# Batch 0's opening of an attention-and-MLP kernel, issued from a written list of pieces

## The chip, the cores and the metric

The kernel runs on one core of one Trainium2 chip. A core has a matrix engine (TensorE, PE in the profile, with weight loads shown as PEld), a vector engine (VectorE, DVE), an activation engine (ScalarE, ACT), a general engine (GpSimd, POOL), and a queue engine (SyncE, SP) that here only issues DMAs. Each engine runs its instructions in the order in which the program issued them and waits on semaphores for the others. PE writes to PSUM, which POOL can't read; DVE and ACT move results from there to SBUF.

The metric is the device time of one execution in microseconds (us). The kernel before took 324.24 us, the median of three runs (324.21 to 324.35).

## The reference

Sliding-window attention over 8 batches of 8 heads, 576 tokens and 64 channels, and then a two-layer perceptron with a leaky ReLU on the 4608 tokens.

```python
scores = (1.0 / np.sqrt(D)) * np.matmul(q, k.transpose(0, 1, 3, 2))     # [8, 8, 576, 576]
mask = np.abs(pos[:, None] - pos[None, :]) <= 32
scores = np.where(mask, scores, -1e9)
attn = exp(scores - max); attn = attn / (attn.sum(-1) + 1e-9)
x = np.matmul(attn, v).transpose(0, 2, 1, 3).reshape(4608, 512)
h = x @ w_in                       # [512, 2048]
out = np.maximum(0.01 * h, h) @ w_out   # [2048, 512]
```

Inputs are float32 and so is the output. The kernel computes in bf16.

## The kernel before

**Tiling.** Two heads make a pair, so each batch has four pairs `p`. A batch's 576 tokens are cut into two halves of 288 (`HALF`). An attention step `i` is one half of one pair: `i = 8*b + 4*half + p`. Steps 0 to 3 are batch 0's first half, steps 4 to 7 its second. The MLP goes by groups `g` of 288 tokens: group 0 needs steps 0 to 3, group 1 needs steps 4 to 7.

**Operands.** `qf`, `kf`, `vf` are float32 tiles as loaded; `qb` and `kb` their casts, 96 tokens on the partitions; `tp` a transposed pair in PSUM; `qT` the transposed queries. `kbd` and `vbd` hold keys and values block-diagonally, so that the two heads of a pair share one matmul; their off-diagonal blocks have to be cleared once. There are two copies of both, for even and odd batches. `win` and `mask` are the 0/1 window.

**One step** consists of: five score matmuls into the single PSUM tile `ps` (line 301); one exponential on ACT into `e` (306); a product with the mask on POOL into `prob` (308); two matmuls with a block of ones for the sums (333); a reciprocal on DVE (338); five matmuls of probabilities with values (352); and a scaling on DVE into `xT` (366). The functions are `score`, `sums`, `product` and `scaled`. There is one buffer for `ps`, one each for `s` and `x`, two for `e`, and four PSUM banks named `mm` that transposes, first-layer and second-layer results share; with `spare`, a step's sums or product take one of these instead.

**The MLP.** `h_tile(g, f)` makes 128 of the 2048 hidden columns: four matmuls over the four pairs of `xT` (line 380) and a Prelu on ACT into `gT` (387). `h_first` interleaves the first four tiles so that the matmuls of pair `c` can run as soon as that pair's `xT` is there. `o_tile` does the second layer (422), an eviction (427) and the store. `keep_busy` (434) issues matmuls whose results nobody reads.

**Order.** The program is in manual schedule: each engine's order is the order of the calls. From line 487 the opening of batch 0 is written out by hand: casts, transposes (`turn_over`, `transpose`, `straight`), masks, scores 0 to 3, then the products; first-layer tiles of group 0 are mixed with steps 4 to 7 in `second_half`. Then group 1's first layer runs while batch 1's queries and keys are cast and transposed (`second_pair`). From there a planner spreads the steps evenly between the MLP's matmuls, by `due` times in estimated microseconds.

**Queues.** SP issues the loads of queries, values and (after batch 0) keys, and the stores. POOL issues, between its computing instructions, DMAs that cast on the way: batch 0's four key loads (line 109), four slices of `w_in` (480) and four of `w_out` (484). `load_early` (101) issues query pair and key pair in turn. The value loads (93) wait on a one-element DVE memset (91), and batch 1's loads (79) on a POOL memset (75); everything behind such a wait on SP waits too.

The parts of the opening that the change touches most are the calls that begin with `cast_q(0, DVE)`:

```python
    cast_q(0, DVE)
    turn_over(0, 0, "q")
    tk0 = transpose(0, 0, "k")
    DVE.memset(kbd[0][:, 2:4], 0.0)
    cast_q(1, DVE)
    straight(0, tk0, ACT, DVE)
    turn_over(0, 1, "q")
    for p in range(NPAIR):
        load_v(0, p, DVE if p == 0 else None)
```

Of the kernel before, what the change touches and what calls it, by code (L numbers as in the profile page):

```python
# [12 lines left out]
ALU = mybir.AluOpType  # L13


@with_exitstack
def kernel(
# [85 lines left out]
    def load_early(p):  # L103

        t = fload.tile([96, 2, RUN * D], FP32, name=f"qf{p}")
        nc.sync.dma_start(out=t, in_=q[0, 2 * p:2 * p + 2].rearrange("a (p c) d -> p a (c d)", c=RUN))
        qf[0, p] = t
        t = kb[:, p].rearrange("p c a d -> p (c a d)").rearrange("p (a c d) -> p a c d", c=RUN, d=D)
        nc.gpsimd.dma_start(out=t, in_=k[0, 2 * p:2 * p + 2].rearrange("a (p c) d -> p a c d", c=RUN))
        early[p] = t  # L110
# [3 lines left out]
    for p in range(NPAIR):  # L114
        load_early(p)
# [13 lines left out]
    def clear(t, p):  # L129
        flat = t[:, p].rearrange("p n j -> p (n j)")  # L130
        nc.scalar.activation(
            out=flat, in_=zero.to_broadcast([128, NB * 128]), func=AF.Copy,
        )
# [14 lines left out]
    w = win[0:64]  # L148
    nc.gpsimd.affine_select(
        out=w, in_=w, compare_op=ALU.is_ge, fill=0.0,  # L150
        base=0, channel_multiplier=-1, pattern=[[1, 2], [0, 3], [2, 64]],
    )
    nc.gpsimd.affine_select(
        out=w, in_=w, compare_op=ALU.is_ge, fill=0.0,
        base=2 * W, channel_multiplier=1, pattern=[[-1, 2], [0, 3], [-2, 64]],
    )
    nc.gpsimd.memset(vbd[0][:, 2], 0.0)
    nc.gpsimd.memset(vbd[0][:, 3], 0.0)
    win_f = win.rearrange("p c m i -> p c (m i)")

    def make_mask(hf):
        lo = (16, 32)[hf]
        nc.vector.tensor_copy(out=mask[hf][:, 0], in_=win_f[:, :, lo:lo + EVEN])
        lo = (16, 0)[hf]
        nc.vector.tensor_copy(out=mask[hf][:, 1, :, lo:lo + 128], in_=win_f[:, :, 0:128])
# [10 lines left out]
    clear(vbd[0], 0)  # L176
    clear(vbd[0], 1)
# [43 lines left out]
    def transpose(b, p, which):  # L221
        tp = mmps.tile([128, RUN, 96], BF16, name="tp", tag="mm")
        for c in range(RUN):
            if b == 0 and which == "k":
# [13 lines left out]
    def straight(p, tp, *engs):  # L238

        for a, eng in enumerate(engs):  # L240
            r = slice(64 * a, 64 * a + 64)
            copy(eng, kbd[0][r, p, :, r], tp[r].rearrange("p c i -> p i c"))

    def cast_q(p, eng):
        copy(eng, qb[:, p], qf[0, p].rearrange("p a (c d) -> p c a d", d=D))

    def evict(b, p, which, tp):
        if which == "q":
            nc.scalar.activation(
                out=qT[b][:, p].rearrange("p (c i e) -> p c i e", c=2, e=RUN // 2),  # L250
                in_=tp.rearrange("p (e c) i -> p c i e", c=2), func=AF.Copy,
# [44 lines left out]
    def score(i):  # L296
        b, hf, p = where(i)
        by_c = qT[b][:, p].rearrange("p (c i) -> p c i", c=2)
        for n_, blocks in enumerate(WIN[hf]):
# [5 lines left out]
        e = attn.tile([128, 2 * HALF], BF16, name="e")  # L305
        nc.scalar.activation(out=e, in_=ps[:, P0:P0 + 2 * HALF], func=AF.Exp, scale=scale)  # L306
        pr = prob[:, i % NPROB]
        nc.gpsimd.tensor_mul(  # L308
            pr.rearrange("p n c i -> p (n c i)"), e, mask[hf].rearrange("p n c i -> p (n c i)"),
        )  # L310
        probs[i] = [pr, None, None]
# [9 lines left out]
    def sums(i, spare=False):  # L321

        b, hf, p = where(i)
        pr, both, _ = probs[i]
# [4 lines left out]
        if both is not None:  # L329
            nc.tensor.matmul(s, ones_bd, both, start=True, stop=True)  # L330
        else:
            for n in range(2):
                nc.tensor.matmul(  # L333
                    s, ones_bd, pr[:, n].rearrange("p c i -> p (c i)"),
                    start=(n == 0), stop=(n == 1),
                )
        r = recip.tile([128, HALF], FP32, name="r")
        nc.vector.reciprocal(r, s)  # L338
        probs[i][2] = r

    def product(i, spare=False):
# [3 lines left out]
        if spare:  # L345
            x = mmps.tile([128, 512], FP32, name="mm", tag="mm")[:, 0:HALF]
        else:
            x = xps.tile([128, HALF], FP32, name="x")
# [7 lines left out]
        probs[i][1] = x  # L356
# [7 lines left out]
    def scaled(i):  # L364
        _, x, r = probs.pop(i)
# [34 lines left out]

    def h_first(g):

        hs = [mmps.tile([128, 512], FP32, name="mm", tag="mm") for _ in range(4)]
        yield hs[0]
        for c in range(DMC):
            for f in range(4):
                h_mms(g, f, hs[f], (c,))
            if c == DMC - 1:
                for f in range(4):
                    h_out(g, f, hs[f])  # L410
            yield
# [75 lines left out]
    ACT, DVE, POOL = nc.scalar, nc.vector, nc.gpsimd  # L487
    cast_q(0, DVE)
    turn_over(0, 0, "q")
    tk0 = transpose(0, 0, "k")  # L490
    DVE.memset(kbd[0][:, 2:4], 0.0)
    cast_q(1, DVE)
    straight(0, tk0, ACT, DVE)
    turn_over(0, 1, "q")
    for p in range(NPAIR):
        load_v(0, p, DVE if p == 0 else None)
    cast_q(2, DVE)
    cast_q(3, POOL)
    DVE.tensor_copy(out=win[64:128], in_=win[0:64])
    make_mask(0)  # L500
    score(0)
    straight(1, transpose(0, 1, "k"), ACT, DVE)
    turn_over(0, 2, "q")
    make_mask(1)
    load_w_in(0, 512)
    score(1)
    sums(0)
    straight(2, transpose(0, 2, "k"), ACT, ACT)
    turn_over(0, 3, "q")
    tk3 = transpose(0, 3, "k")  # L510
# [171 lines left out]
```

## Time and profile before

| what | value |
|---|---|
| median of three runs | 324.24 us |
| the profiled execution | 323.54 us |
| its span, first to last instruction | 321.8 us |
| first transposes of queries on PE | 4.40 us |
| first scores, step 0 (line 301) | 9.27 us |
| first matmuls of line 380 | 25.42 us |
| memset that releases batch 1's loads (line 75) | 28.32 us |
| end of the last scaling of batch 0 (line 366) | 39.33 us |
| first matmuls of the second layer (line 422) | 48.25 us |
| PE busy in 12 to 16, 16 to 20, 20 to 24, 24 to 28 us | 3.94, 2.75, 2.38, 4.00 us |

The span counts from the first instruction to the last; the time of the run has 1.74 us more around it. A row of the instruction timeline gives start, length, engine, line, operation and tiles, and in brackets the idle time before it and what ended that. "PE busy" is modelled from pipelined matmuls, so a busy PE isn't PE at its best rate. The chain of waits follows the end of the span back, step by step, to what released each piece of work.

### The profile page before, as it was taken

What the parts mean: (1) busy time and instruction counts of PE and PEld (TensorE: products, weight loads), DVE (VectorE), ACT (ScalarE), POOL (GpSimd) and SP (SyncE); (2) the same over time, 40 slices, a digit from 0 to 9 for tenths busy, and PEclk for the clock granted to TensorE, in tenths of its full rate; (3) what the DMA queues carried; (4) which work ended last, traced back from release to release, by engine and by line L of the source; (5) the groups of instructions that cost most, each with busy time, mean ns of one, the idle gap of its engine ahead of it and who ended that gap; (6) DMA issues with size and microseconds to landing.
All of it is one profiled execution on the core that took longest, in us unless ns stands there. A gap on an engine that the chain in (4) does not pass through costs nothing.

```text
span 321.8 us, 6484 instructions
## 1 busy us (share of the span) xinstructions
PE 304.6 (95%) x2448; PEld 206.2 (64%) x2468; DVE 218.2 (68%) x261; ACT 181.4 (56%) x392; POOL 190.7 (59%) x247
## 2 busy tenths in 40 slices
PE   2769998999999999999999999999999999999995
PEld 1547784576674857676665857676665858576753
DVE  5757956769836888588846988588745987565100
ACT  5656598755552837465552837465552837463631
POOL 8768955875537856586537866586637866330000
PEclk9999999999999999999999999999999999999999
DMA  8799999998999999389834997499933440010101
GB/s 196 141 155 159 255 266 204 228 200 181 186 235 197 219 234 223 69 218 216 188 74 91 230 233 165 70 206 203 206 75 103 109 68 35 33 37 6 60 35 66
DMA packets 108400, 48.87 MB, mean 152 GB/s; under 512 B 68816, under 2 KB 103888, under 8 KB 108368
## 3 DMA queue, kind: packets, MB, share of 16 engines
q1 hardware_dynamic: 103312, 43.66, 64.8%
q0 software_dynamic: 5056, 4.78, 9.5%
q8 instruction: 19, 0.31, 0.4%
q14 instruction: 13, 0.11, 0.1%
HBM read 36.70 MB, written 9.44 MB: 143 GB/s over the span
## 4 chain that ended last, share of the span: by engine, by line
PE 90%; ACT 2%; DVE 2%; DMA 2%; issue 2%; POOL 1%; POOLq 0%; ACTq 0%; DVEq 0%
PE mm L380 39%; PE mm L422 38%; PE ps L301 5%; PE x L352 5%; PE s L330 2%; DMA kb<-in_k_dram 2%; DVE r L338 1%; PE s L333 1%; ACT vbd L206 1%; POOL prob L308 1%; ACT e L306 1%; PE tp L229 1%; DVE kbd L236 0%; ACT kbd L234 0%; PE ps L434 0%
## 5 line engine op out<-in xcount | busy, mean ns | idle before, releaser
L338 DVE RECIPROCAL r<-s 128x288 f32<-128x288 f32 x63 | 123.3, 1957 | 57.6 <-PE s L330 52.9
L308 POOL TENSOR_TENSOR prob<-e,mask 128x576 bf16<-128x576 bf16 x64 | 81.4, 1272 | 91.3 <-issue 44.7
L380 PE MATMUL mm<-xT,w_in_bf 128*128 128x288 bf16 x1024 | 135.0, 287 | 0.1
L422 PE MATMUL mm<-w_out_bf,gT 128*128 128x512 bf16 (+2 forms) x572 | 128.7, 373 | 1.1
L380 PEld LDWEIGHTS <-w_in_bf 128*128 128x128 bf16 x1024 | 98.8, 98 | 25.0 <-issue 0.3
L387 ACT ACTIVATE gT<-mm 128x288 bf16<-128x288 f32 x256 | 101.2, 412 | 24.1 <-PE mm L380 7.7
L422 PEld LDWEIGHTS <-gT 128*128 128x128 bf16 x592 | 56.3, 98 | 59.2
L427 ACT ACTIVATE o_sb<-mm 128x512 f32<-128x512 f32 (+2 forms) x37 | 21.7, 585 | 92.0 <-PE mm L422 92.0
L306 ACT ACTIVATE e<-ps 128x576 bf16<-128x576 f32 x64 | 41.5, 648 | 15.6 <-PE ps L301 15.4
L208 POOL CAST vbd<-vf 64x576 bf16<-64x576 f32 x51 | 35.0, 685 | 1.5
L366 DVE TENSOR_TENSOR xT<-x,r 128x288 bf16<-128x288 f32 x63 | 28.8, 457 | 8.5 <-PE x L352 2.4
L199 POOL CAST kb<-kf 96x384 bf16<-96x384 f32 (+1 forms) x52 | 31.0, 619 | 5.0 <-DMA kf<-in_k_dram 5.0
L286 DVE COPY kbd<-kT 64x576 bf16<-64x576 bf16 x48 | 32.0, 667 | 1.0 <-DMA kT<-kb 0.7
L301 PE MATMUL ps<-qT,kbd 128*128 128x128 bf16 (+2 forms) x320 | 27.2, 219 | 1.9 <-DVE kbd L236 1.9
L301 PEld LDWEIGHTS <-kbd 128*128 128x128 bf16 x320 | 21.6, 102 | 11.2 <-DVE kbd L236 2.3
L352 PE MATMUL x<-prob,vbd 128*128 128x64 bf16 (+1 forms) x315 | 26.0, 214 | 1.1 <-ACT vbd L206 0.9
L199 POOL CAST qb<-qf 96x384 bf16<-96x384 f32 x48 | 24.4, 536 | 0.0
L352 PEld LDWEIGHTS <-vbd 128*128 128x128 bf16 x320 | 21.1, 100 | 5.2 <-ACT vbd L206 3.1
L318 DVE TENSOR_TENSOR both<-prob 128x288 bf16<-128x288 bf16 x52 | 20.3, 391 | 0.9
L330 PE MATMUL s<-both,ones_bd 128*128 128x288 bf16 x52 | 14.9, 286 | 0.0
L206 ACT ACTIVATE vbd<-vf 64x576 bf16<-64x576 f32 x13 | 8.8, 679 | 0.3
L229 PE MATMUL tp<-ident,qb 96*128 96x96 bf16 x48 | 4.3, 241 | 4.4 <-DVE qb L236 4.4
(57 smaller groups left out, 89.8 us busy)
## 6 DMA issues: line engine op xcount, KB each, us to landing
qf<-in_q_dram SPq DMA_DIRECT2D x32, 288.0 KB, 4.6
vf<-in_v_dram SPq DMA_DIRECT2D x64, 144.0 KB, 4.1
out_dram<-o_sb SPq DMA_DIRECT2D x35, 256.0 KB, 4.1
kf<-in_k_dram SPq DMA_DIRECT2D x28, 288.0 KB, 4.9
w_in_bf<-in_moe_w_in_dram POOLq DMA_DIRECT2D x4, 512.0 KB, 5.5
w_out_bf<-in_moe_w_out_dram POOLq DMA_DIRECT2D x4, 512.0 KB, 15.2
kb<-in_k_dram POOLq DMA_DIRECT2D x4, 144.0 KB, 6.8
qT<-qb SPq DMA_TRANSPOSE x24, 4.3
```

The costliest lines, as they stand in the source:

```text
L199: eng.tensor_copy(out=to, in_=tok)
L208: eng.tensor_copy(out=vbd[b % 2][r, p, :, r], in_=vf[b, p][r])
L286: nc.vector.tensor_copy(out=to.rearrange("p n (m c) -> p n c m", c=2), in_=kT[r].rearrange("p (c n m) -> p n c m", c=2, n=NB),)
L301: nc.tensor.matmul(ps_v[:, n_, :, i0:i0 + n], kbd[b % 2][:, p, blk], by_c[:, :, hf * EVEN + i0:hf * EVEN + i0 + n], start=True, stop=True,)
L306: nc.scalar.activation(out=e, in_=ps[:, P0:P0 + 2 * HALF], func=AF.Exp, scale=scale)
L308: nc.gpsimd.tensor_mul(pr.rearrange("p n c i -> p (n c i)"), e, mask[hf].rearrange("p n c i -> p (n c i)"),)
L338: nc.vector.reciprocal(r, s)
L352: nc.tensor.matmul(x_v[:, :, i0:i0 + n], vbd[b % 2][:, p, blk, :], pr[:, n_, :, i0:i0 + n], start=(blk == parts[0][1]), stop=(blk == parts ...
L366: nc.vector.tensor_mul(place(i), x, r)
L380: nc.tensor.matmul(h[:, 0:HALF], w_in_bf[:, c, ts(f, 128)], xT[:, c, ds(g * HALF % RING, HALF)], start=(c == 0), stop=(c == DMC - 1),)
L387: nc.scalar.activation(out=gT[:, f, ds(g * HALF % RING, HALF)].rearrange("p (i c) -> p i c", c=2), in_=h[:, 0:HALF].rearrange("p (c i) -> ...
L422: nc.tensor.matmul(o[:, lo:hi], gT[:, f, ds(128 * j % RING, 128)], w_out_bf[:, f, lo:hi], start=(f == 0), stop=(f == FFC - 1),)
```

## The change

`load_early` takes no pair any more. SP's queue now carries query pair 0, key pair 0 as float32, then query pairs 1 to 3, and straight after these the eight value loads, with no memset ahead of them. POOL's queue carries only key pairs 1 to 3. Key pair 0 is cast by an engine and transposed like a query pair.

Clearing `vbd[0]` and the second half of `kbd[0]`, which lines 157, 158, 176, 177 and 491 of the old order did at fixed places, becomes pieces `zk` and `zv` of the list. The copy of the window to the upper partitions is done on ACT instead of DVE.

The hand-written calls from `cast_q(0, DVE)` through `second_half` and group 0's first layer to `h_first(1)` are replaced by a list of 154 named pieces with an engine each; an engine's order is the list's order. `score` is split in `score_mms` (S), `exps` (X) and `masked` (M), `sums` in `sum_mms` (B) and `recips` (R); P is a product and U a scaling. Fillers are one of four and one of three matmuls, where there were four of four. `H0c`/`H1c` are a group's first four tiles for one pair, `H0_f` and `E0_f` a tile's matmuls and its Prelu, `f` the clears of the odd batches' `kbd` and `vbd`, `gate` the memset with batch 1's loads. The clears of `vbd[1]` pairs 2 and 3 inside group 1's first layer stay as well.

```diff
+OPENING = [
+    "zk2:ACT zv2:DVE zk3:ACT win:POOL zv1:DVE cq0:DVE zv0:POOL winc:ACT tq0:PE ck0:DVE eq0:ACT mask0:DVE",
+    "zv3:POOL tk0:PE cq1:DVE kA0:ACT tk1:PE mask1:POOL kB0:ACT tq1:PE kA1:DVE S0:PE cq2:ACT eq1:DVE",
+    "tk2:PE X0:ACT kB1:DVE cq3:POOL tq2:PE kA2:ACT M0:DVE S1:PE eq2:ACT kB2:DVE B0:PE X1:ACT tq3:PE",
+    "R0:DVE cv00:POOL S2:PE M1:POOL eq3:ACT tk3:PE X2:ACT cv01:POOL kA3:ACT B1:PE M2:DVE wi0:POOL kB3:ACT",
+    "P0:PE R1:DVE B2:PE cv11:ACT wi1:POOL S3:PE cv20:ACT cv10:POOL U0:DVE X3:ACT cv21:POOL P1:PE R2:DVE",
+    "cv30:ACT S4:PE M3:POOL P2:PE fill4:PE X4:ACT cv31:ACT S5:PE fill3:PE wi2:POOL U2:DVE B3:PE X5:ACT",
+    "U1:DVE wi3:POOL P3:PE R3:DVE S7:PE M5:POOL H0c0:PE H0c1:PE H0c2:PE wo0:POOL X7:ACT U3:DVE B5:PE",
+    "M4:DVE H0c3:PE f7:POOL R5:DVE P4:PE E0_0:ACT S6:PE E0_1:ACT wo1:POOL P5:PE E0_3:ACT H0_4:PE E0_2:ACT",
+    "gate:POOL wo2:POOL E0_4:ACT H0_5:PE U5:DVE X6:ACT B4:PE M7:DVE wo3:POOL H0_6:PE E0_5:ACT R4:DVE",
+    "M6:POOL H0_7:PE E0_6:ACT H0_8:PE E0_7:ACT H0_9:PE E0_8:ACT f3:POOL H0_10:PE E0_9:ACT U4:DVE B6:PE",
+    "E0_10:ACT f2:POOL P6:PE R6:DVE H0_11:PE H0_12:PE E0_11:ACT f4:POOL H0_13:PE E0_12:ACT H0_14:PE",
+    "E0_13:ACT U6:DVE f0:POOL B7:PE E0_14:ACT H0_15:PE R7:DVE f1:POOL P7:PE E0_15:ACT H1c0:PE f6:POOL",
+    "H1c1:PE U7:DVE H1c2:PE f5:POOL H1c3:PE",
+]
+SPARE_SUMS, SPARE_PRODUCTS = (0, 1, 2), (0, 1, 5)
...
+    def load_early():
+        for into, src, name, p in ((qf, q, "qf", 0), (kf, k, "kf", 0), (qf, q, "qf", 1), (qf, q, "qf", 2), (qf, q, "qf", 3)):
+            t = fload.tile([96, 2, RUN * D], FP32, name=f"{name}{p}")
+            nc.sync.dma_start(out=t, in_=src[0, 2 * p:2 * p + 2].rearrange("a (p c) d -> p a (c d)", c=RUN))
+            into[0, p] = t
+        for p in range(1, NPAIR):
+            t = kb[:, p].rearrange("p c a d -> p (c a d)").rearrange("p (a c d) -> p a c d", c=RUN, d=D)
+            nc.gpsimd.dma_start(out=t, in_=k[0, 2 * p:2 * p + 2].rearrange("a (p c) d -> p a c d", c=RUN))
+            early[p] = t
+        for p in range(NPAIR):
+            load_v(0, p)
...
-    nc.gpsimd.memset(vbd[0][:, 2], 0.0)
-    nc.gpsimd.memset(vbd[0][:, 3], 0.0)
...
-    clear(vbd[0], 0)
-    clear(vbd[0], 1)
...
-            if b == 0 and which == "k":
+            if b == 0 and which == "k" and p > 0:
...
+    def h_open(g):
+        hs[g] = [mmps.tile([128, 512], FP32, name="mm", tag="mm") for _ in range(4)]
...
+        elif kind == "M":
+            masked(n, eng)
+        elif kind == "B":
+            sum_mms(n, n in SPARE_SUMS)
+        elif kind == "P":
+            product(n, n in SPARE_PRODUCTS)
+        elif kind == "gate":
+            load_next(eng)
+        elif kind == "fill":
+            keep_busy(idle["bank"], HALF, n)
+        elif kind == "f":
+            eng.memset((kbd if n < 4 else vbd)[1][:, n % 4], 0.0)
...
+    for item in " ".join(OPENING).split():
+        name, eng = item.split(":")
+        one(name, ENGINE[eng])
+    state["done"] = 2 * NPAIR
...
     cast_qk(1, 0, nc.vector)
     cast_qk(1, 1, nc.vector)
-    for _ in h_first(1):
-        pass
+    for f in range(4):
+        h_out(1, f, hs[1][f])
```

## The prediction

> **What bounds the kernel now.** I read the page first, then busy time by stage, then the chain of waits, then the opening by engine.
>
> ```profile
> span 321.8 us, 6484 instructions
> PE 304.6 (95%) x2448; PEld 206.2 (64%) x2468; DVE 218.2 (68%) x261; ACT 181.4 (56%) x392; POOL 190.7 (59%) x247
> ```
>
> TensorE is busy for 95% of the span, and what it lacks lies almost wholly at the start. In the busy times below (columns: length, PE busy and count, granted clock, DMA share, GB/s), PE is some 73% busy per window until 24.55 us and gapless after.
>
> ```profile
> 14.30:17.70 3.40, 2.60 (x26) 1.00 1.05 166
> 17.70:21.15 3.45, 2.35 (x16) 1.00 0.88 136
> 21.15:24.55 3.40, 2.44 (x21) 1.00 1.04 155
> 24.55:27.97 3.42, 3.42 (x21) 1.00 1.06 156
> ```
>
> The chain of waits shows both what the opening waits for and the clock (start, length, what):
>
> ```profile
> 1.58 5.41 DMA kb<-in_k_dram
> 7.04 0.71 PE tp L226 x12
> ...
> 25.63 1.92 PE mm L380 x8
> ...
> 31.73 1.96 PE mm L380 x16
> ```
>
> The first keys hold the start until 7.04. Eight matmuls of line 380 take 1.92 at 25.63 (0.24 each), sixteen take 1.96 at 31.73 (0.1225 each): TensorE runs at half rate until about 28.0. The column of granted clock says 1.00 throughout and can't be used there. After 28 the opening's last steps hang on VectorE (start, length, engine, line):
>
> ```profile
> 13.21 1.96 DVE L338 RECIPROCAL r<-s 128x288 f32<-128x288 f32 x1 [0.53 <-PE s L333]
> 16.39 1.96 DVE L338 RECIPROCAL r<-mm 128x288 f32<-128x288 f32 x1 [1.22 <-PE mm L333]
> ...
> 25.67 1.96 DVE L338 RECIPROCAL r<-s 128x288 f32<-128x288 f32 x1 [0.77 <-PE s L333]
> ...
> 38.87 0.46 DVE L366 TENSOR_TENSOR xT<-x,r 128x288 bf16<-128x288 f32 x1
> ```
>
> From the first reciprocal (13.21) to the end of the eighth scaling (39.33) are 26.1 us; eight reciprocals of 1.96 and eight scalings of 0.46 fill 19.4, so 6.7 are waits. The last scaling releases the last four matmuls of the second half's first group, which end near 40.0. What follows is the same code in both kernels, on a gapless TensorE, so the end moves with that point if the loads of batch 1 move too.
>
> **The change, part by part.** I walk the list in order on each engine, with 0.09 between a producer and its consumer (kernel before: scores end 9.91, exponential starts 10.00).
>
> **First keys.** Key pair 0 takes second place on SP's queue, where query pair 1 landed at 1.23 + 3.3 = 4.5; I take 4.7. Key pairs 1 to 3 move up a place on POOL's queue: 7.0, then 8.9 and 10.6 because SP's queue carries more bytes beside them (before 8.4, 9.8, 10.6). Query pairs 1 to 3 are pushed back to 6.1, 8.0, 10.0. One more cast (0.56 alone, 1.13 beside a busy POOL) goes to DVE. If SP's queue gains nothing, the cover of the next part leaves a loss of 0.7.
>
> **The window mask.** What sets the first scores is now another chain. POOL issues three key loads (1.58 to 3.75 at 0.73), then two selects:
>
> ```profile
> 3.79 0.56 DVE L236 CAST qb<-qf 96x768 bf16<-96x768 f32 x1 [0.57 <-DMA qf<-in_q_dram]
> ...
> 4.48 0.55 POOL L149 TENSOR_SCALAR_AFFINE_SELECT win<-win 64x384 bf16<-64x384 bf16 x1
> ...
> 5.10 1.90 POOL L153 TENSOR_SCALAR_AFFINE_SELECT win<-win 64x384 bf16<-64x384 bf16 x1
> 5.47 1.13 DVE L236 CAST qb<-qf 96x768 bf16<-96x768 f32 x1
> ```
>
> The same select takes 0.55 alone and 1.90 beside a cast. Now two casts run beside the second: between 1.5 and 3.2; I take 2.2, nearest the 1.90, so it ends at 6.5. In list order follow the copy of the lower half on ACT (0.5, by the 0.57 of a 64x576 one), mask0 on DVE (0.45), and only then the cast of query pair 1 (0.85, between 0.56 and 1.13), the transposes of it, and S0, at 9.1 (before 9.27). So waiting ACT holds eq0, and waiting DVE holds cq1. The earlier keys are nearly used up here. The bounds of the select move the end by -0.1 to +0.7, those of the casts by ±0.3.
>
> The Trainium skill's page "SBUF — State Buffer", section "Who interferes with whom", speaks against piling casts on DVE here: a fast DVE copy and a GpSimd instruction exclude each other for whole instructions. By it both casts would hold the select, ending it near 7.2 and adding about 0.5 to the end; the rows of 0.55 and 1.90 agree in kind.
>
> **First half.** Exponential 0 at 9.8; its mask product moves from POOL (1.27) to DVE. A 128x576 product on DVE is not in the trace; the nearest row is the 128x288 sum of line 318 at 0.39, so 0.4 to 0.8; I take 0.72. Reciprocals then start at 12.4, 15.1, 17.5 and 20.9 (before 13.21, 16.39, 19.63, 25.67). R3 comes 4.8 earlier since scores 4 to 7 no longer stand ahead of it as they did, and U1 ends at 20.5 with no cold filler between: fillers drop from 16 matmuls to 7. Clearing of the value tiles leaves ACT for DVE and POOL, and the key tiles' second half goes to ACT; this is hidden before 7 us, where ACT waits for the window.
>
> **Clock.** The walk finds TensorE without a gap over 0.3 from 17.5 on. Before, it was gapless from 22.1 and reached full rate 5.9 later; by this row full rate comes at 23.4. Bounds: 20.9, if a stretch as long as the one wholly busy window above (3.4) is enough, and 26.8, if it takes one such more than 5.9; they move the end by -0.3 and +1.3.
>
> The page "TensorE: Matmul & The Clock Gate", Part 1, has the clock released after one busy window of about 3.4 us that runs free of the kernel; that would be 20.9 to 24.3 here, and the sum would be lower by up to 0.3.
>
> **Second half.** From R3 at 20.9 DVE has five reciprocals (9.8), five scalings (2.3), two mask products (1.4) and about 1.1 of waits for TensorE: U7 ends at 35.5, where it ended at 39.33. Counted the other way: DVE starts 0.8 sooner, its waits fall from 6.7 to 1.6, and three mask products add 2.2: 3.8 saved. I take off 0.3 for one more stretched copy (the mask copy took 0.51 and 0.23). ACT's sixteen activations end at 33.9 and POOL's clears at 36.5; neither binds. POOL clears all eight tiles now and two of them again later, where it waited 2.97 us for keys before.
>
> **Loads.** SP's five query and key issues (0.44 each) end by 3.1 and eight value issues (0.64 each) by 8.3, without the gate at 9.26 and with nothing due behind them until batch 1; the mean DMA share was 0.55 from 8 to 12 us, so they fill a hole. I count 4608 packets at about 800 per us after 9.7 (trace's DMA records), landing 11.7 (pair 0) to 15.9 (pair 3). Weight slices issue at 14.4, 15.2, 18.8 and 19.6 (before 12.40 to 26.06) and land by 20, 22.5, 25 and 28, ahead of use at 21.6 and later. Batch 1's loads are released by a POOL memset, at 28.32 before and 24.6 now: 3.7 earlier, as is the compute. They landed from 36.0 to 50.1, and POOL waited for them, so this matters as much.
>
> **Sum.** 3.8 - 0.3 = 3.5. Span 321.8 - 3.5 = 318.3. The profiled run took 323.54, 1.74 beside the span, and the median is 0.70 above it: 324.24 - 3.5 = 320.7.
>
> **Rivals.**
> *Values starved (slower).* In the profile before, weight slice 0 issued at 12.4 stopped the values: in the two us from 15 the trace counts 345 weight packets against 33 of values, and the last value load took 7.9:
>
> ```profile
> vf<-in_v_dram SPq DMA_DIRECT2D x1, 144.0 KB, 7.9
> ```
>
> Now slice 0 (14.4 + 1.9) starts 0.8 after I have the values' last packet, and slice 1 is right behind. If pair 3 is caught, it lands at 22.6 as before, and cv30 on ACT, at 17.4 in the walk, holds exponentials 4, 5 and 7 and all behind them for 5.2: 5.2 - 3.5 = 1.7 slower, 325.9. It decides from a landing near 20.9. Against it: slice 0 stands on POOL behind cv00, M1 and cv01, so late values delay it too.
> *Batch 1's loads hold.* They flowed first at 32.9, 4.5 after the issue, once weight packets gave way. With all four output-weight slices now queued around the gate, they could wait for all of these: 2424 packets at 202 per us, to 36.6. Queries and keys of pair 0 then land at 38.4 and 39.3, and TensorE waits some 1.8 for their transposes: 3.5 - 1.8 = 1.7 saved, 322.5. Against it, before they alternated one to one from 33 on with weight packets queued.
> *Clock missed.* Full rate at 26.8 costs 1.3 (322.0); only one near 33 brings the end back to 40. Fewer fillers speak for it, the dense walk against.
> *The keys don't come sooner:* 321.4.
>
> **How the numbers follow.** Forecast 0.62; values starved 0.17; loads hold 0.10; clock 0.07; keys no sooner 0.04. Differences below 0.2% (0.65 us) can't be told from none. Faster: 0.62, nearly all of the loads, clock and keys cases, and a small part of half-caught values: 0.82; same 0.04; slower 0.14. The forecast's own bounds (gains 2.2 to 4.5) give 319.7 to 322.0. For 8 in 10: low 319.4, where select, casts and clock all fall well; up to 323.6, which holds the two lesser rivals and leaves out the starved values and some of the same.
>
> **What would show it.** Right: S0 near 9, R3 near 21, matmuls of 0.12 from about 23.4, last scaling of batch 0 ending near 35.5, gate near 24.6, keys of batch 1 landing some 4 sooner. Wrong: exponential 4 after 21 beside a late value cast; transposes of batch 1 waiting for its loads; 0.24 matmuls past 27; or a steady state after 60 us that takes back what the opening gave.

## The result, and the profile after

The changed kernel takes 321.06 us, the median of four runs (319.78 to 322.44), against 324.3 us for the kernel before in the same session (four runs, 324.21 to 324.76). The ratio is 0.9898, 95% interval [0.9849, 0.9947]: faster by 1.0%. The same code run again in a later session gave 320.5 us and 0.9866 [0.9839, 0.9893]. In the first session the four runs of the kernel before lie within 0.55 us and those of the changed one spread over 2.7 us. The later sessions show that the change doesn't bring this spread: with 10 to 20 runs each, and one slow run left out, the kernel before spreads over 1.9 to 4.6 us there (323.13 to 326.33 in the one with 20).

The profiled execution of the changed kernel is the slowest of its four, 322.44 us. Its page, first line and engine line:

```profile
span 320.7 us, 6477 instructions
PE 303.8 (95%) x2453; PEld 203.6 (63%) x2453; DVE 221.3 (69%) x264; ACT 180.7 (56%) x391; POOL 188.2 (59%) x247
```

The span fell by 1.1 only, in this execution. Busy times in the same four stretches (length, PE, PEld, DVE, ACT, POOL, granted clock, DMA share, GB/s):

```profile
14.30:17.70 3.40, 2.56 (x24) 1.50 (x20) 3.18 (x4) 3.21 (x6) 3.29 (x5) 1.00 0.62 104
17.70:21.15 3.45, 3.06 (x27) 2.85 (x28) 1.95 (x2) 2.61 (x5) 3.31 (x5) 1.00 1.07 176
21.15:24.55 3.40, 2.97 (x28) 1.96 (x27) 3.06 (x5) 1.08 (x2) 3.35 (x4) 1.00 1.06 165
24.55:27.97 3.42, 3.29 (x36) 2.73 (x36) 3.32 (x6) 2.69 (x8) 2.75 (x6) 1.00 1.23 201
```

TensorE is busier between 17.70 and 24.55 than it was (3.06 and 2.97 against 2.35 and 2.44), and in the last stretch it issues 36 matmuls where 21 filled it before: the clock has come up sooner. Rows of the timeline, all engines, show when, and what became of the opening's steps:

```profile
4.29 0.95 POOL L178 TENSOR_SCALAR_AFFINE_SELECT win<-win 64x384 bf16<-64x384 bf16 x1
5.20 2.04 POOL L157 MEMSET vbd<- 128x1152 bf16 x2
5.25 2.40 DVE L258 CAST kb<-kf 96x768 bf16<-96x768 f32 x1 [0.41 <-DMA kf<-in_k_dram]
...
12.04 0.82 POOL L258 CAST qb<-qf 96x768 bf16<-96x768 f32 x1 [3.77 <-DMA qf<-in_q_dram]
...
12.97 1.96 DVE L374 RECIPROCAL r<-mm 128x288 f32<-128x288 f32 x1
...
20.62 0.72 PE L466 MATMUL x<-mask,ones_bd 128*128 128x224 bf16 x3
21.18 0.41 PE L366 MATMUL s<-prob,ones_bd 128*128 128x288 bf16 x2
...
21.38 0.46 DVE L410 TENSOR_TENSOR xT<-x,r 128x288 bf16<-128x288 f32 x1 [1.73 <-PE x L466]
...
22.12 1.95 DVE L374 RECIPROCAL r<-s 128x288 f32<-128x288 f32 x1
...
34.91 0.46 DVE L410 TENSOR_TENSOR xT<-x,r 128x288 bf16<-128x288 f32 x1
```

Two sums matmuls took 0.69 at 16.31 and take 0.41 at 21.18: full rate starts at 21.17 by the trace's clock records, where the kernel before reached it at 27.97. The last scaling of batch 0 ends at 35.37 instead of 39.33, 3.96 sooner. The first matmul of the second layer starts at 43.85 instead of 47.81, again 3.96. So the opening gave 4.0 us, and the run as a whole gave 1.1 in this profile. (The table ahead of the prediction gives 48.25 for that matmul; in the timeline of the kernel before it starts at 47.81.) The chain of waits shows where the difference began (start, length, what):

```profile
2.74 9.24 DMA qf<-in_q_dram
...
12.04 0.83 POOL qb L258
...
15.82 1.51 POOL w_in_bf L512 x2
...
25.53 6.11 DMA qf<-in_q_dram
...
31.66 17.22 DMA vf<-in_v_dram
...
48.96 0.68 ACT vbd L228
```

Up to 50 us the chain no longer has a reciprocal of VectorE in it (the chain of before had one, 29.06 to 31.03). It goes through the loads: the fourth query pair, POOL's queue with the weight issues and the gate, then batch 1's loads up to 48.9. At that point TensorE waits in its timeline, first for the output weights and then for a value copy on ACT:

```profile
48.45 1.02 PE L454 MATMUL mm<-w_out_bf,gT 128*128 128x512 bf16 x4 [1.06 <-DMA w_out_bf<-in_moe_w_out_dram]
...
50.40 0.41 PE L396 MATMUL x<-prob,vbd 128*128 128x96 bf16 x5 [0.45 <-ACT vbd L228]
```

The kernel before has one such wait in its own timeline:

```profile
53.76 0.41 PE L352 MATMUL x<-prob,vbd 128*128 128x96 bf16 x5 [0.94 <-ACT vbd L206]
```

1.06 + 0.45 - 0.94 = 0.57 is given back here. Up to there the loads flow at the same rate in both kernels, 267 to 268 GB/s. Two stretches of the kernel before and two of the changed one (columns as above):

```profile
36.00:40.00 4.00, 4.00 (x38) 2.99 (x36) 3.77 (x5) 1.62 (x5) 4.00 (x5) 1.00 1.16 267
40.00:44.00 4.00, 3.87 (x41) 3.16 (x40) 2.04 (x3) 3.82 (x12) 2.36 (x3) 1.00 1.16 268
```

```profile
32.00:36.00 4.00, 3.64 (x32) 2.67 (x31) 3.64 (x5) 1.52 (x5) 4.00 (x5) 1.00 1.16 268
36.00:40.00 4.00, 3.87 (x40) 3.14 (x39) 0.93 (x3) 3.82 (x11) 1.83 (x2) 1.00 1.16 268
```

By the trace's packet records the last packet of the output weights ends at 50.43 before and at 48.02 now: 2.4 sooner, while TensorE wants it 3.96 sooner. I follow the rest by the evictions of the second layer on ACT (37 of them in each trace): how much earlier each one starts than in the profile of before. This "lead" is 3.36 at the first eleven (53.7 to 122 us in the time of before) and 0.70 at all that follow (the tail behind the last one is another 0.4 shorter, which makes up the 1.1). A second loss of 2.65 thus lies in one place. DVE's and PE's rows there:

```profile
115.58 1.93 DVE L307 COPY kbd<-kT 64x576 bf16<-64x576 bf16 x2 [2.69 <-DMA kT<-kb]
...
120.05 0.28 PE L363 MATMUL s<-both,ones_bd 128*128 128x288 bf16 x1 [1.24 <-DVE r L374]
```

The transposed keys, issued at 110.06, landed 5.5 us later; DVE waits for them 2.69 with the next reciprocals behind it, and TensorE runs out of work (busy 2.81 of the 4 us from 116). The second profile of the same kernel (below) doesn't have this loss at all.

### The profile page after: what moved, and what is told of

Same layout as the page of the kernel before. It is cut to its first block, busy times and chain, and to the rows that moved or that the text cites. A ratio compares the mean times of both kernels' runs of the same rounds, so it can differ in the third digit from the quotient of the medians.

```text
span 320.7 us, 6477 instructions
## 1 busy us (share of the span) xinstructions
PE 303.8 (95%) x2453; PEld 203.6 (63%) x2453; DVE 221.3 (69%) x264; ACT 180.7 (56%) x391; POOL 188.2 (59%) x247
## 4 chain that ended last, share of the span: by engine, by line
PE 72%; DMA 12%; POOL 8%; DVE 4%; issue 3%; SPq 1%; ACT 1%; DVEq 0%; POOLq 0%; ACTq 0%
PE mm L454 32%; PE mm L424 31%; DMA vf<-in_v_dram 5%; DMA qf<-in_q_dram 5%; PE x L396 4%; PE ps L322 3%; POOL prob L336 2%; DVE r L374 2%; DMA kT<-kb 2%; PE s L363 2%; POOL kb L221 1%; POOL qb L221 1%; DVE kbd L307 1%; POOL w_in_bf L512 1%; POOL vbd L230 1%
## 5 line engine op out<-in xcount | busy, mean ns | idle before, releaser
L374 DVE RECIPROCAL r<-s 128x288 f32<-128x288 f32 x61 | 119.3, 1955 | 54.7 <-PE s L363 51.6
L454 PE MATMUL mm<-w_out_bf,gT 128*128 128x512 bf16 (+2 forms) x592 | 130.4, 374 | 1.1 <-DMA w_out_bf<-in_moe_w_out_dram 1.1
L336 POOL TENSOR_TENSOR prob<-e,mask 128x576 bf16<-128x576 bf16 x60 | 76.4, 1274 | 88.6 <-issue 42.9
L230 POOL CAST vbd<-vf 64x576 bf16<-64x576 f32 x52 | 36.2, 696 | 1.6
L307 DVE COPY kbd<-kT 64x576 bf16<-64x576 bf16 x48 | 33.2, 691 | 3.2 <-DMA kT<-kb 2.7
L410 DVE TENSOR_TENSOR xT<-x,r 128x288 bf16<-128x288 f32 x61 | 27.9, 458 | 7.9 <-PE x L466 1.7
L396 PE MATMUL x<-prob,vbd 128*128 128x64 bf16 (+1 forms) x305 | 24.8, 213 | 1.5 <-DVE xT L410 0.9
## 6 DMA issues: line engine op xcount, KB each, us to landing
w_out_bf<-in_moe_w_out_dram POOLq DMA_DIRECT2D x4, 512.0 KB, 17.5
```

The costliest lines, as they stand in the source:

```text
L230: eng.tensor_copy(out=vbd[b % 2][r, p, :, r], in_=vf[b, p][r])
L307: nc.vector.tensor_copy(out=to.rearrange("p n (m c) -> p n c m", c=2), in_=kT[r].rearrange("p (c n m) -> p n c m", c=2, n=NB),)
L336: eng.tensor_mul(pr.rearrange("p n c i -> p (n c i)"), es.pop(i), mask[hf].rearrange("p n c i -> p (n c i)"),)
L374: nc.vector.reciprocal(r, probs[i][2])
L396: nc.tensor.matmul(x_v[:, :, i0:i0 + n], vbd[b % 2][:, p, blk, :], pr[:, n_, :, i0:i0 + n], start=(blk == parts[0][1]), stop=(blk == parts ...
L410: nc.vector.tensor_mul(place(i), x, r)
```

## The experiments

All were timed beside runs of the kernel before (324.38 to 324.49 us). "Lead" is used as above, against the one profile of before; that execution was 0.7 us below its median, so a lead in a profile understates the gain over that median by about that much. A lead is that of one execution, and its clock is too: in the profiles of the changed kernel and its variants the clock is full at times from 15.69 to 23.24. The four executions with full rate by 17.4 (experiments 4, 7, 9 and 12) took 318.62 to 319.91 us; those with full rate from 20.6 to 21.2 took 320.02 to 320.45, or 322.44 with the loss at 112 us; the one with 23.24 took 322.49 (experiment 2, which loses time elsewhere, is left out). So a difference of leads between two kernels can be one between two executions, and the medians decide.

**1. The changed kernel again.** No edit.

> The changed kernel, unaltered, to see the spread of its executions (319.78 to 322.44 in four). Theory A (the opening gives 3.4 for certain; one late DMA transpose of batch 2's keys at about 110 us gives up to 2.7 back in some executions): times fall between 319.5 and 322.5, spread out or in two clusters, and every profile has the evictions of the second layer 3.4 ahead of the kernel before until 97 us, whatever the total. Rival B (the clock of the opening is reached at a different time in each execution): the lead would differ already at 60 us. Rival C (chance of measurement): spread under 1 us now.

Measured: 320.5 us (318.57 to 320.89, six runs), ratio 0.9866 [0.9839, 0.9893]. The lead is 2.67 at every one of the 37 evictions, so theory A's 3.4 didn't come. The lead differs from the first eviction on, as rival B had it, but not for its reason: the clock was full at 21.02 here and at 21.17 there. The loss at 112 us belongs to the first execution and not to the kernel; the wait for the output weights is there again, and longer, in PE's timeline:

```profile
49.28 1.02 PE L454 MATMUL mm<-w_out_bf,gT 128*128 128x512 bf16 x4 [1.85 <-DMA w_out_bf<-in_moe_w_out_dram]
```

**2 and 3. The key copies one step later**, in the changed kernel and in the one before. If a late transpose only hurts because DVE stands waiting for it, a later place should give it slack.

```diff
-        landing.append((8 * (b - 1) + 4 + p, b, p, kT))
+        landing.append((8 * (b - 1) + 5 + p, b, p, kT))
```

> Only the step at which VectorE copies the transposed keys into place is one later for batches 2 to 7, so a transpose may land some 4 us later before VectorE waits for it. Theory A: the give-back disappears; all executions 319.4 to 320.3, median 319.8 or less, spread under 1 us. Rival B or C: spread and median stay as in the changed kernel (319.8 to 322.4, median near 321). If the copies one step later are themselves in the way of VectorE's reciprocals: median above 321.

> The same delay of the copies in the kernel before, where VectorE waited 0.7 us for a transpose once and nothing followed from it. Theory A: no change, 324.0 to 324.5. If the copies' place matters by itself, a change beyond 0.65 us.

Measured: 323.49 us (322.6 to 325.1), 0.9975 [0.9957, 0.9994] with the change, and 328.12 (326.92 to 329.23), 1.0115 [1.0093, 1.0138] without it: both expectations failed, each kernel lost 3 to 4 us. The lead falls from 3.12 in four steps, of 0.4 and then about 0.95 each, until the kernel is 0.13 behind. A pair's copy now is issued in the step just ahead of the one that issues its scores, and TensorE waits for it in its timeline, in four of the six batches:

```profile
119.60 0.41 PE L322 MATMUL ps<-qT,kbd 128*128 128x96 bf16 x5 [0.38 <-DVE kbd L307]
```

The place of that copy has no slack on either side: later it stalls the scores, and where it is, it stalled DVE when the transpose was late. This says nothing on what makes a transpose late.

**4. A shift of TensorE's instruction stream**: 15 small idle matmuls at the start. In the first profile a 16 KB packet of the instruction queue (at 112.1, 1.60 us long) lay beside 256-byte transpose packets that took up to 1.47 us; the shift moves such packets relative to the transposes.

```diff
+    for _ in range(15):
+        nc.tensor.matmul(ps[:, 0:64], ones_bd, ones_bd[:, 0:64], start=True, stop=True, skip_group_check=True)
```

> The changed kernel with 15 more small matmuls on an idle TensorE at the start (30 more instructions of it, results unused), which moves the points at which its instructions are fetched by 16 KB DMAs by some 2 us against the rest. Theory A with the fetch as the cause of the late transpose (the fetch at 112.1 us met transposes of 256-byte packets that took up to 1.5 us): the stall near 112 goes or changes, and with it the spread; median away from 321.1 by 0.7 or more, either way. Rival D (the fetch has no part, the load and store traffic does it): same distribution as the changed kernel.

Measured: 320.06 us (319.72 to 320.39), 0.9866 [0.9845, 0.9887]; lead 3.40 throughout, no loss at 112. The time is 1.0 under the 321.1 that the theory had started from, as it asked. But run 1 had no such loss either, without the shift, and its instruction packet at 111.8 also lay beside transpose packets of up to 1.37 us. So the packets coincide in executions with and without the loss; that they cause it is not shown. The clock was full at 15.69 here, which can't be put down to the idle matmuls (experiment 7 had 17.08 without them); the opening ended 1.2 sooner than in run 1 (34.22 against 35.42), and the wait for output weights (1.30) took part of that back.

**5. The new loads alone in the kernel before** (SP's order, key pair 0 as float32, values with no gate; the old order of work with one cast more).

```diff
+    copy(DVE, kb[:, 0], kf[0, 0].rearrange("p a (c d) -> p c a d", d=D))
...
-    for p in range(NPAIR):
-        load_v(0, p, DVE if p == 0 else None)
```

> The kernel before with the change's loads alone: key pair 0 second on SP's queue as float32 and cast on VectorE, the value loads right after the queries, the rest of the hand-written order kept. Theory (the gain comes from the list's order, and the new loads by themselves push query pair 3 back to about 12 us, where POOL's cast of it stands ahead of mask product 0, and let weight slice 0 starve the last values): no gain or slower, 324.2 to 326.5. Rival (the earlier keys are the gain): 321 to 323.

Measured: 324.36 us (323.69 to 326.89), 0.9997 [0.9976, 1.0019]. The loads by themselves give nothing, as the theory had it: here too the cast of the keys is stretched beside POOL's clears and query pair 3 arrives late, as DVE's and POOL's rows show, and with the old order the last scaling ends at 39.93. The converse, the list with all the old loads, wasn't run; so what the list gives is shown together with the new loads.

```profile
5.08 2.43 DVE L239 CAST kb<-kf 96x768 bf16<-96x768 f32 x1 [0.38 <-DMA kf<-in_k_dram]
...
12.13 0.82 POOL L239 CAST qb<-qf 96x768 bf16<-96x768 f32 x1 [5.03 <-DMA qf<-in_q_dram]
```

**6. Key pair 0 back on POOL's queue**, cast by its DMA, in the changed kernel (`ck0` and the `kf` load leave, POOL loads all four pairs).

```diff
-        for into, src, name, p in ((qf, q, "qf", 0), (kf, k, "kf", 0), (qf, q, "qf", 1), (qf, q, "qf", 2), (qf, q, "qf", 3)):
+        for into, src, name, p in ((qf, q, "qf", 0), (qf, q, "qf", 1), (qf, q, "qf", 2), (qf, q, "qf", 3)):
...
-        for p in range(1, NPAIR):
+        for p in range(NPAIR):
```

> The changed kernel with key pair 0 back on POOL's casting queue, ahead of the other three, and without its cast on VectorE. The recorded prediction's rival priced the keys coming no sooner at 0.7 slower. Theory after the trace (the earlier key was spent on a cast that POOL's clears stretched to 2.40 us, and it pushed query pair 3 to 12.0, which held POOL for 3.77 us): not slower, the first scores near 9.5 to 10, query pair 3 before 10, the last scaling of batch 0 0.3 to 1.5 sooner, median 0 to 1 below the changed kernel's 320.5. Rival (the key's place is what pays): 0.7 or more slower.

Measured: 322.47 us (319.89 to 322.9; of nine runs six lie from 322.31 to 322.9, two near 319.9 and one at 320.75), 0.9917 [0.9886, 0.9948]. Slower by about 2 in the median, as the rival had it and not the theory. Query pair 3 was cast at 9.72, but the first scores came at 10.97 and the clock was full only at 23.24. The opening is only 0.54 later (last scaling ends at 35.91). The profile, from the upper cluster, has the wait for output weights at its latest place (to 49.74), and after it TensorE falls back to half rate for one window (length, PE to POOL, granted clock, DMA share, GB/s):

```profile
47.14:50.55 3.41, 1.57 (x18) 0.95 (x16) 0.90 (x2) 1.69 (x3) 2.25 (x2) 1.00 1.14 193
50.55:53.96 3.41, 3.41 (x18) 1.89 (x17) 2.04 (x2) 3.29 (x6) 0.00 (x0) 0.50 1.03 201
```

The lead drops by 1.24 there (2.26 to 1.02). This doesn't explain the upper cluster: the mean granted clock recorded with each run is 0.994 for the profiled one, but 1.000 for 322.31, 322.47 and 322.61, so these three have no half-rate window after the clock first came up; 319.89 in the lower cluster has 0.995. Why six of nine runs are some 2 us longer stays open.

**7. The key cast on ACT**, ahead of the copy of the window.

```diff
-    "zk2:ACT zv2:DVE zk3:ACT win:POOL zv1:DVE cq0:DVE zv0:POOL winc:ACT tq0:PE ck0:DVE eq0:ACT mask0:DVE",
+    "zk2:ACT zv2:DVE zk3:ACT win:POOL zv1:DVE cq0:DVE zv0:POOL ck0:ACT winc:ACT tq0:PE eq0:ACT mask0:DVE",
```

> The changed kernel with the cast of key pair 0 on ScalarE ahead of the window copy, away from the collision with POOL's clears. Theory: cast 0.8 instead of 2.4, first scores about 1 us sooner (near 8.8), but query pair 3 still lands at 12, so the first reciprocals gain at most 0.5 and the last scaling and the total stay within 0.5 of the changed kernel's 320.5. Rival (the first scores set the opening): 0.7 to 1 faster.

Measured: 320.07 us (319.01 to 322.17), 0.9875 [0.9836, 0.9914]. On ACT, beside the same two clears on POOL, the cast takes 0.84, as its row shows:

```profile
5.40 0.84 ACT L256 ACTIVATE kb<-kf 96x768 bf16<-96x768 f32 x1 [0.75 <-DMA kf<-in_k_dram]
```

That is 1.56 less than on DVE, and it is worth next to nothing: the first scores start at 9.59 against 9.83 (8.8 expected), the first reciprocal at 13.30, not sooner, and the last scaling ends at 35.25 against 35.37. The two longest runs (321.86 and 322.17) have a mean granted clock of 0.993; where in them it fell isn't recorded.

**8. No fillers.**

```diff
-    "cv30:ACT S4:PE M3:POOL P2:PE fill4:PE X4:ACT cv31:ACT S5:PE fill3:PE wi2:POOL U2:DVE B3:PE X5:ACT",
+    "cv30:ACT S4:PE M3:POOL P2:PE X4:ACT cv31:ACT S5:PE wi2:POOL U2:DVE B3:PE X5:ACT",
```

> The changed kernel without its seven filler matmuls. Theory: full TensorE rate comes one window later (near 24.5 instead of 21.1) and the last scaling of batch 0 some 1 us later, but the first second-layer tile waits for the last slice of the output weights anyway (1.1 to 1.9 us in the profiles), so the total moves by less than 0.7: 320.2 to 321.3. Rival (the opening's end sets the total): 1 to 1.5 slower, 321.5 to 322. Rival (fillers have no part in the clock): last scaling unmoved.

Measured: 319.89 us (319.47 to 320.41), 0.9854 [0.9823, 0.9886]; clock full at 21.19, as with them, so the later clock of the theory didn't come. The seven idle matmuls have no part in the gain; they cost the opening something. They are written into the tile `x` that the scaling of step 2 reads next, and VectorE waits until the last of them is done: 1.73 in the row at 21.38 above, 1.07 in run 1. Without them the fourth reciprocal starts at 20.90 in place of 22.12 and the last scaling ends at 34.70 in place of 35.37:

```profile
20.14 0.46 DVE L410 TENSOR_TENSOR xT<-x,r 128x288 bf16<-128x288 f32 x1
20.51 0.45 DVE L410 TENSOR_TENSOR xT<-mm,r 128x288 bf16<-128x288 f32 x1
20.90 1.96 DVE L374 RECIPROCAL r<-s 128x288 f32<-128x288 f32 x1
```

Of this 0.7 the median can't show much: 0.6 below experiment 1, with overlapping runs.

**9. The first weight slice earlier, values of pair 3 later** (`wi0:POOL` ahead of `cv00:POOL`, `cv30:ACT` behind `X4:ACT`), to draw the output weights forward.

```diff
-    "R0:DVE cv00:POOL S2:PE M1:POOL eq3:ACT tk3:PE X2:ACT cv01:POOL kA3:ACT B1:PE M2:DVE wi0:POOL kB3:ACT",
+    "R0:DVE wi0:POOL cv00:POOL S2:PE M1:POOL eq3:ACT tk3:PE X2:ACT cv01:POOL kA3:ACT B1:PE M2:DVE kB3:ACT",
...
-    "cv30:ACT S4:PE M3:POOL P2:PE fill4:PE X4:ACT cv31:ACT S5:PE fill3:PE wi2:POOL U2:DVE B3:PE X5:ACT",
+    "S4:PE M3:POOL P2:PE fill4:PE X4:ACT cv30:ACT cv31:ACT S5:PE fill3:PE wi2:POOL U2:DVE B3:PE X5:ACT",
```

> The changed kernel with weight slice 0 issued before the first value cast on POOL (near 12.9 instead of 15.8) and value cast 30 moved behind exponential 4 on ScalarE, where a late value pair 3 can't hold it. Theory W (the end is set at 48 to 49 us, where TensorE waits 1.0 to 1.9 for the last slice of the output weights, and that slice is late because the weight stream starts only at 17.7 after a hole of 1.3 in the DMAs): the last slice lands 1.2 or more sooner, the wait shrinks below 0.5, and the total falls by 0.5 to 1.3 to 319.2 to 320, although the opening's vector work ends about 0.8 later. Rival V (weights starve the values): value pairs 2 and 3 land 2 us later, ScalarE or POOL waits for them, and the total is 320.5 or more. Rival O (the opening's end sets the total): 0.8 slower, 321.3.

Measured: 320.64 us (319.91 to 321.65), 0.9882 [0.9859, 0.9905]. The wait for the output weights is gone, and TensorE waits for keys and values instead:

```profile
47.98 0.43 PE L251 MATMUL tp<-ident,kb 96*128 96x96 bf16 x6 [0.48 <-POOL kb L221]
...
50.56 0.41 PE L396 MATMUL x<-prob,vbd 128*128 128x96 bf16 x5 [0.81 <-ACT vbd L228]
```

So the wait shrank as theory W had it, and the total didn't fall. The values of batch 0 did land later, as rival V had it (last packet at 19.4 against 16.7, by the packet records), but none of their copies shows a wait and the opening ended sooner, at 34.47. The expectation had misread the stream that it starts from: the changed kernel's first weight packet is at 17.3, after a hole of 0.6.

**10. The gate behind the third output slice.**

```diff
-    "gate:POOL wo2:POOL E0_4:ACT H0_5:PE U5:DVE X6:ACT B4:PE M7:DVE wo3:POOL H0_6:PE E0_5:ACT R4:DVE",
+    "wo2:POOL gate:POOL E0_4:ACT H0_5:PE U5:DVE X6:ACT B4:PE M7:DVE wo3:POOL H0_6:PE E0_5:ACT R4:DVE",
```

> The changed kernel with the release of batch 1's loads after output-weight slice 2's issue instead of before it, 0.75 later. Theory W: the last output slice lands 0.5 to 0.7 sooner and the keys of pair 3 as much later; the wait of TensorE for the weights shrinks, that for the keys grows from nothing by less; total 0 to 0.6 lower. Rival (batch 1's keys and values set the total): 0.5 to 0.8 slower, 321 to 321.3.

Measured: 319.81 us (319.36 to 320.24), 0.9856 [0.9833, 0.988]; the wait for weights is 1.11, between the 1.06 and 1.85 of the unaltered kernel's two profiles, so that it shrank isn't shown; that for the value copy is 0.82 (0.45 and 0.29).

**11. Experiments 7, 9 and 10 together.**

> Slice 0 early, the cast of value pair 3 behind exponential 4, the release after slice 2, and the cast of key pair 0 on ScalarE, all in one. Theory W: opening and weight stream both sooner, 318.5 to 319.6 and below each single edit; a faster version than both kernels. If one of the edits turns out to harm, near or above 320.

Measured: 320.33 us (319.96 to 321.24), 0.9878 [0.9856, 0.9899]; lead 3.08. Missed: the three don't add up. The wait for output weights is gone, and TensorE waits for keys (0.85 ahead of the second layer, 0.22 in it) and for a value copy (0.81): the edits changed which load comes last.

**12. A quarter of the output weights not loaded.** The quarter is cleared at the end of the list instead, so the output lacks the last quarter of the hidden columns.

```diff
-    "gate:POOL wo2:POOL E0_4:ACT H0_5:PE U5:DVE X6:ACT B4:PE M7:DVE wo3:POOL H0_6:PE E0_5:ACT R4:DVE",
+    "gate:POOL wo2:POOL E0_4:ACT H0_5:PE U5:DVE X6:ACT B4:PE M7:DVE H0_6:PE E0_5:ACT R4:DVE",
...
-    "H1c1:PE U7:DVE H1c2:PE f5:POOL H1c3:PE",
+    "H1c1:PE U7:DVE H1c2:PE f5:POOL wo3:POOL H1c3:PE",
...
         c = slice(4 * i, 4 * i + 4)
+        if i == 3:
+            nc.gpsimd.memset(w_out_bf[:, c, :], 0.0)
+            return
         nc.gpsimd.dma_start(out=w_out_bf[:, c, :], in_=w_out_r[:, c, :])
```

> The changed kernel without the load of the last quarter of the output weights (1 MB fewer to fetch; that quarter of w_out_bf is cleared on POOL at the end of the opening instead, so that the last quarter of the hidden columns adds nothing to the output). The number of matmuls is the same. Theory, the loads between 29 and 49 us fill the DMA engines and whichever lands last sets the end: the waits of TensorE at 48 to 51 us for w_out, keys and values of batch 1 vanish or fall below 0.3, the second layer's evictions run 3.8 to 4.5 ahead of the kernel before instead of 2.7 to 3.4, and the time falls to 318.6 to 319.8. Rival, what the opening gained is lost elsewhere (in TensorE's own queue or in VectorE): the waits on loads vanish but others take their place, the lead stays at 2.7 to 3.4 and the time at 320.2 to 321.2.

Measured: 319.79 us (318.62 to 321.19), 0.9849 [0.9805, 0.9893]. The profiled execution, 318.62, has a lead of 4.48 at every eviction, the largest of all; experiment 8, whose opening ends only 0.26 later, has 2.67. No wait for weights is left, and the one left is for ACT, which makes its value copies without waiting for a load:

```profile
49.28 0.41 PE L396 MATMUL x<-prob,vbd 128*128 128x96 bf16 x5 [1.09 <-ACT vbd L228]
```

The lead is as the theory had it, and so is the wait for weights; a wait for values stays, 1.09 against 0.94 in the kernel before. The median isn't: it is at the edge of what the theory gave, 0.7 below experiment 1 with overlapping runs, and no better than experiments 8 and 10. So the removed wait shows in the profiled execution, which is the fastest of the six and had its clock full at 16.99 (21.19 in experiment 8); in the medians it isn't shown.

**Together.** The profiles give this account (us). "Opening" is the end of batch 0's last scaling, "first" how much earlier than before the second layer's first matmul starts, "waits" those of TensorE for weights, keys and values listed from there to 51 us, less the 0.94 of before, and "lead" is read at 53.7.

| kernel | opening | first | waits | first - waits | lead |
|---|---|---|---|---|---|
| changed, first profile | 35.37 | 3.96 | 0.57 | 3.39 | 3.36 |
| 1, changed, again | 35.42 | 3.90 | 1.20 | 2.70 | 2.67 |
| 2, copies later | 34.78 | 4.54 | 1.35 | 3.19 | 3.12 |
| 4, idle matmuls | 34.22 | 4.40 | 0.68 | 3.72 | 3.40 |
| 6, keys on POOL's queue | 35.91 | 3.41 | 0.90 | 2.51 | 2.26 |
| 7, key cast on ACT | 35.25 | 4.08 | 0.05 | 4.03 | 4.08 |
| 8, no fillers | 34.70 | 4.04 | 1.19 | 2.85 | 2.67 |
| 9, first slice earlier | 34.47 | 3.57 | 0.35 | 3.22 | 3.20 |
| 10, gate later | 34.90 | 4.23 | 1.19 | 3.04 | 2.86 |
| 11, three together | 34.89 | 3.19 | 0.09 | 3.10 | 3.08 |
| 12, a quarter not loaded | 34.44 | 4.47 | 0.15 | 4.32 | 4.48 |

The opening doesn't order the lead: three openings that end within 0.25 of each other (34.22 to 34.47) have leads from 3.20 to 4.48. The start of the second layer less the waits gives the lead to within 0.2 in nine of the eleven rows, and to 0.25 and 0.32 in the other two.

## Why the prediction was right, point by point

The forecast, 3.5 us from an opening that ends 3.8 sooner, held: 324.3 - 321.06 = 3.2, and 320.7 was 0.4 from the median. Its mechanism, a list that lets VectorE's eight reciprocals run with fewer waits and an earlier clock, is what the profile shows: from the first reciprocal (12.97) to the end of the eighth scaling (35.37) are 22.4 us, and eight reciprocals, eight scalings and three mask products of 0.45 leave 1.7 of waits, where 6.7 stood before and 1.6 was forecast. How much of this the order gives and how much the clock, no run separates. Several terms were wrong and cancelled; that the total came so close is partly luck.

- *First keys.* They landed near 5.2 (4.7 forecast). The push of the other loads was undersized: the fourth query pair came at 11.98, 9.24 after its issue, not at 10.0, and POOL stood idle 3.77 for it; SP's eight value issues ended at 14.09, not at 8.3. Key pair 1 was there at 8.7, not 7.0.
- *The window mask* was sized with the wrong victim. I let the casts hold the second select to 6.5 (2.2 long); it took 0.95 and ended at 5.24. It was the cast of the keys that was held, 2.40 against the 0.56 to 1.13 that I had. It starts 0.05 after POOL's two clears and ends 0.41 after them. I had called these clears hidden; they weren't. The two errors cancel in part, and scores 0 started at 9.83 (9.1 forecast, 9.27 before). The Trainium skill's page "SBUF — State Buffer", section "Who interferes with whom", which in the prediction stood for an even later select, adds that the order of issue decides who blocks. The rows of this case agree that one of the two waits, but it isn't always the one whose row starts later. The second select began ahead of the cast of the queries (4.29 against 4.35), and it was the select that was stretched, while the cast took 0.49. In experiments 4, 8, 9, 10 and 12 the cast of the keys begins 0.13 to 0.23 ahead of the clears and is held all the same, to 0.41 to 0.43 after their end. From experiment 9:

```profile
5.04 2.62 DVE L258 CAST kb<-kf 96x768 bf16<-96x768 f32 x1 [0.20 <-DMA kf<-in_k_dram]
...
5.20 2.04 POOL L157 MEMSET vbd<- 128x1152 bf16 x2
```

  In experiment 5, with the clears first (5.05 to 7.10), the cast starts at 5.08 and ends at 7.51, again 0.41 later. In experiment 2 the cast of the keys met the second select instead (5.09 against 5.31) and took 0.56. So in the profiles of the changed kernel a cast on DVE is held by POOL's clears and not by its selects, whichever begins first; why is open.
- *First half.* A 128x576 mask product on DVE takes 0.46, not 0.72. Reciprocals started at 12.97, 15.52, 17.70 and 22.12, for 12.4, 15.1, 17.5 and 20.9. The fourth was late because U2 waited 1.73 for the fillers: the walk had them out of the way, and without them it starts at 20.90 (experiment 8).
- *Clock.* Full at 21.17, not 23.4: near the lower bound of 20.9, and inside the 20.9 to 24.3 that the prediction worked out from the Trainium skill's page "TensorE: Matmul & The Clock Gate", Part 1. In experiment 8 it came at 21.19 without the fillers. The nine variants of the changed kernel that were profiled and its two own profiles give the clock a bounded part in the gain: their full rates lie 7.6 us apart (15.69 to 23.24) and their openings 1.7 (34.22 to 35.91), the later clock mostly beside the later opening (17.08 beside 35.25, and 21.19 beside 34.70 without fillers, are out of order). As an estimate from these, a clock that is 6.8 earlier than before gives about 1.5 of the 3.96; the edits differ too, so this isn't shown.
- *Second half.* Last scaling at 35.37 (35.5 forecast), from a fourth reciprocal that was 1.2 late: mask products of 0.45 and almost no waits, where I had 0.7 and 1.1, made up for it. That the clock was early may be why the waits were short.
- *Values starved* fell. By the trace's packet records the values' last packet was at 16.7 (15.9 forecast) and the weights' first one at 17.3. Weight slice 0 was issued at 15.77 rather than 14.4, since POOL had waited for the fourth query pair: the same delay protected the values. Experiment 9 issued it at 12.50: the last values came 2.7 later, and the opening lost nothing.
- *The keys don't come sooner.* So it was in fact: landing 0.5 late, then a cast of 2.40, so that the first key transposes started at 7.71 (7.04 before). Alone the new loads gave nothing (experiment 5). That the total didn't lose the 0.7 of this rival is due to what came after. Putting the pair back on POOL's queue wasn't priced right either: 0.54 of opening, and about 2 in the median, mostly by what came after.
- *What follows is the same code on a gapless TensorE, so the end moves with the opening if the loads of batch 1 move too.* This is the step that failed in part: the loads didn't move as far as the compute. The gate moved by 2.9 (28.32 to 25.42), not 3.7, and the loads behind it go through DMA engines that run at the same rate in both kernels: 267 to 268 GB/s and a DMA share of 1.16 in the windows from 32 to 44 us, and from 36 to 48 in the kernel before. The last output weights landed 2.4 sooner, not 3.96. The rival *Batch 1's loads hold* had the place nearly right (the output-weight slices against batch 1's loads) and the price too high: 0.57 and 1.20 in the two profiles, for 1.8. What TensorE waits for is mostly the last output slice, at 48 to 49 us, not the first transposes.
- *A steady state that takes back what the opening gave* happened in one execution, 2.65 at 112 to 122 us. The sum had no term for it. It belongs with the spread of the runs.

What stays open: why a key transpose took 5.5 us in one execution, how often that happens, why most runs of experiment 6 are 2 us longer, and what else makes the runs of either kernel spread.

## What to carry to other kernels

When an opening is shortened, list the first loads that its successors need and see how full the DMA engines are up to there: here the load that came last took back 0.6 to 1.2 of 4.0 us, and reordering the loads only changed which one that was. Where a vector cast and a general-engine instruction overlap, price both as the one that waits: here a clear held the cast and a select didn't, and which began first made no difference. Look where idle matmuls write: here a scaling waited for them. And compare two profiles of the same kernel, and the spread of the kernel before in several sessions, before explaining a loss that only one of them shows.

## What the hardware showed that I had not expected

- A float32 to bf16 cast of 96x768 on DVE took 1.98 to 2.68 beside POOL's memsets (2.40 in the changed kernel's first profile, 2.59 to 2.68 where it began ahead of them), where it takes 0.49 to 0.56 without; ACT did it in 0.84 beside the same memsets.
- The clock came to full rate at times from 15.69 to 23.24 in kernels that differ by a few instructions (15.69, 16.99, 17.08, 17.39, 20.63, 21.02, 21.17, 21.19, 23.24 are some). The profiled executions with the earlier clock were the shorter ones, 318.62 to 319.91 us with full rate by 17.4; the medians of their kernels, over other executions, aren't in that order.
- One window of 3.41 us with TensorE busy 1.57 of it was followed by a window at half rate, long after the start (experiment 6).
- DMAs of 288 KB that land in 4.4 us at the median in the first 16 us of the kernel before took 7.1 in the changed kernel, with a fifth such load among them and the value loads directly behind on the same queue.
